# Starting the paired 64-step form two units earlier, in a linear-attention and SwiGLU kernel

## The chip, the cores and the metric

The kernel runs on one core of one Trainium2 chip. The metric is the time of one execution on the device in microseconds (us), taken as the median of several runs. A profile is one further execution, in which each engine's instructions are recorded. Five engines have a queue of their own, worked off in order: TensorE (PE in the profile, its weight loads PEld), VectorE (DVE), ScalarE (ACT), GpSimd (POOL) and SyncE (SP, which here only issues DMAs). Engines wait for each other by semaphores.

## The reference: what is computed

Two blocks follow each other. The first is a recurrence over 768 steps for 4 batches and 8 heads of 48 elements; its output becomes 3072 rows of 384, which go through a gated feed-forward block with 1536 hidden columns.

```python
for t in range(S):
    kt, vt, rt = (k[:, :, t], v[:, :, t], r[:, :, t])
    cur = np.einsum('bhd,bhe->bhde', u[None] * kt, vt)
    y[:, :, t] = np.einsum('bhd,bhde->bhe', rt, state + cur)
    state = w[None, :, :, None] * state + np.einsum('bhd,bhe->bhde', kt, vt)
...
g = x @ w_gate
silu = g * (1.0 / (1.0 + np.exp(-g)))
val = x @ w_val
return (silu * val @ w_out).astype(np.float32)
```

## The kernel before

**Units.** The recurrence is done in chunks. A chunk of one batch needs the products of all pairs of its steps (scores, masked so that only earlier steps count), the sum over these with `v` plus what the state gives (outputs), and the state's own change (update). The work is cut into 24 units of 128 tokens, numbered in the order in which they are done. Before the change, units 0 to 11 are chunks of 128 steps of one batch, the first three chunks of each of the four batches (`c, b = divmod(i, 4)`). Units 12 to 23 have another form, called paired here: 64 steps of two batches, one in partitions 0 to 63 and one in 64 to 127. `PAIRED` is the number of the first paired unit, and `part(i, p)` tells batch and first step of half `p`.

**The two forms on TensorE.** A plain unit has scores in line 494, outputs in line 645 (a product with the state tile `zs` and one with `v`) and the state's update in line 658. A paired unit has scores in line 546, outputs in line 580 (state and `v` lie in the same tile `v_ld`, so one product covers both) and the update in line 594. Each of `v_ld2` and `v_ld3` (printed by the listings of the instructions as `v_ld_107` and `v_ld_108`) holds, in the paired form, 64 steps of `v` of batch 2 or 3 in half of the partitions and that batch's state in the other half.

**The state of a paired unit.** After the update's matmuls, VectorE adds the result onto the state in `v_ld` (line 610, two instructions for each batch), and GpSimd multiplies the state by the decay (line 613, one for each batch). The next unit of the same two batches reads this state in its outputs. From unit 12 on, batches 0 and 1 take turns with batches 2 and 3, so a state that unit `i` leaves is read by unit `i + 2`.

**The order of the work.** A loop over steps `s` issues everything in program order, and each engine works off its own instructions in this order. In step `s` stand, among others:
- at its top, on GpSimd, `scale_k(s+1)` (line 353) and `own_product(s+1)` (lines 264 and 267);
- `gaps(s, 0)` to `gaps(s, 4)`, five places at which pieces of the feed-forward block are issued by `feed`; each piece is a few matmuls with what belongs to them on the other engines;
- between `gaps(s, 0)` and `gaps(s, 1)`, for paired units, `outputs(s-2)`, then `scores(s-1)` with the update of unit `s-2`; for plain units the scores come first.

Small things of the attention are put into queues and taken out one or two at each `feed`: `small` holds ScalarE's instructions for the term with `u`, `lazy` holds the masked copies of the scores (lines 502 and 554), the two transposes of the next unit (`turn_block`, on VectorE) and the four additions with the two multiplications of the state (lines 610 and 613). What is left of both queues is issued before the next step's scores.

**The feed-forward block.** At first it is done plainly (`gate_value`, line 688). From the tenth step on, the projections use sums of weights and of hidden columns that save matmuls: `weight_sum` (line 717), `h_sums` (lines 740 to 745) and `project` (line 768). From the thirteenth on, three groups of weights are combined as well (`in_place` in line 860, `w_forms` in line 887, both on GpSimd, and the matmuls in line 957).

**DMAs of a paired unit.** `move_blocks` issues eight DMAs from SyncE that rearrange `hats` (line 435; a plain unit has four, line 419), `fill_turned` and `fill_own` fill parts of `At` (lines 524 and 530), `load_v` loads `v` (line 153). The state of the plain form is copied once into `v_ld` (line 675).

Of the kernel before, what the change touches and what calls it, by code (L numbers as in the profile page):

```python
# [12 lines left out]
AF = mybir.ActivationFunctionType  # L13
ALU = mybir.AluOpType
AX = mybir.AxisListType
P = 128
# [6 lines left out]
def fast(  # L23
# [25 lines left out]
    B, H, S, D = r.shape  # L49
# [15 lines left out]
    dve, pool, act, pe, sp = nc.vector, nc.gpsimd, nc.scalar, nc.tensor, nc.sync  # L65
# [17 lines left out]
    NR = 2 * FC  # L83
# [15 lines left out]
    def take():  # L99
# [3 lines left out]
    own = zs[:].rearrange("p b x -> p (b x)")[:, 0 : 2 * H * 64].rearrange(  # L103
        "p (i h t) -> p i h t", i=2, h=H
    )
    r_ld = [cst.tile([P, H, D], FP32, name=f"r_ld{i}") for i in range(2)]
    k_ld = [cst.tile([P, H, D], FP32, name=f"k_ld{i}") for i in range(2)]

# [17 lines left out]
            return khat[i][:, :, 0:D], rhat[i % 2][:, :, 0:D]  # L126
        return k_ld[i % 2][:], r_ld[i % 2][:]

    PAIRED = 12

    def part(i, p):

        c, q = divmod(i - PAIRED, 2)
        return 2 * q + p, PAIRED // B * P + 64 * c

    def pieces_of(i):

# [189 lines left out]
    for l in range(7):  # L327
        n = 1 << l
# [19 lines left out]
    def slot(i, h):  # L348

        return h if i % 2 else H - 1 - h  # L350
# [20 lines left out]
    def diagonal(i, on_act=None):  # L371

        du = dus.pop(i)
        if i >= PAIRED:
            small.extend(
                lambda h=h: act.activation(  # L376
                    own[:, i % 2, slot(i, h), :], ident64, AF.Identity, scale=du[:, h : h + 1]
                )
                for h in range(H)
            )  # L380
            return
        on_act = on_act or (HP if i < 4 else H)
        small.extend(
            lambda h=h: act.activation(
                At[i % 2][:, h, :], ident[:], AF.Identity, scale=du[:, h : h + 1]
            )
            for h in range(on_act)
        )
        if on_act < H:
            n = H - on_act  # L390
            pool.tensor_mul(
                At[i % 2][:, on_act:H], ident[:].unsqueeze(1).to_broadcast([P, n, P]),
                du[:, on_act:H].unsqueeze(2).to_broadcast([P, n, P]),
            )
# [88 lines left out]
    lazy = deque()  # L483
# [29 lines left out]
    def both(i):  # L513

        return At[i % 2][:].rearrange("p h t -> p (h t)").rearrange(
            "p (o h t) -> p o h t", o=2, h=H
        )
# [8 lines left out]
    def fill_own(i):  # L526

        for p in range(2):
            here = slice(64 * p, 64 * p + 64)
            act.dma_start(out=both(i)[here, p], in_=own[here, i % 2])  # L530

    def paired_scores(i, ps):

# [769 lines left out]
    summed = []  # L1303
    todo = []

    def feed(n, pops=1):
        for _ in range(n):
            ready = [k for k, (need, _) in enumerate(todo) if need <= done["pool"] + len(summed)]
            if ready:
                todo.pop(ready[0])[1]()  # L1310
            for _ in range(min(len(lazy), 1 + (len(lazy) > 9))):
                lazy.popleft()()
            for _ in range(min(pops, len(small))):
                small.popleft()()
# [22 lines left out]
    def gaps(s, n):  # L1337

        if s not in EARLY:
            if n == 0:  # L1340
                coming = 40 * ((s < 14) + (s < 18)) + 14 * (s < 22)
                share[0] = -(-(len(todo) + coming) // max(25 - s, 1))
            feed(
                share[0] // 5 + (n < share[0] % 5) - (n == 1 and BLOCKS <= s < PAIRED),
                1,
            )
            return
        for what in EARLY[s][n]:
            if what == "R":
                if done["pool"] < NW:  # L1350
                    round_weights()
                elif len(summed) < 4:
                    weight_sum()
            else:
                feed(1, 3)

    share = [0]
    BLOCKS = 10
    LATE = 12
    EARLY = {s: ("" if s < 7 else "R", "F", "R", "F", "RF") for s in range(5, 12)}  # L1360
    EARLY[4] = ("R", "F", "", "F", "F")

    def flush():
# [89 lines left out]
    for s in range(4, N + 2):  # L1453
        if 4 < s <= PAIRED:
            own_sum(s)
        if s == PAIRED:
            diagonal(s)
        late = BLOCKS < s + 1 < N and s % 2 == 0
        if s + 3 == PAIRED:

            for e in range(2):
                rows, o = slice(64 * e, 64 * e + 64), 64 - 64 * e
                act.copy(mask64[rows], mask[rows, 0, 64 * e : 64 * e + 64])
                act.copy(ident64[rows], ident[rows, 64 * e : 64 * e + 64])
                sp.dma_start(out=w64[rows, :, 1 - e], in_=w64[o : o + 64, :, 1 - e])
        if s + 1 == BLOCKS:
            turn(s)
        if s + 1 < N:
            scale_k(s + 1)
            if s < PAIRED and not late:  # L1470
                scale_r(s + 1)
            own_product(s + 1)
            if s + 1 < BLOCKS:
                load_v(s + 1)
            if s < PAIRED and s + 3 < N and not late:
                load(s + 3)
        if s + 1 < BLOCKS:
            turn(s)
        gaps(s, 0)
        if s > N:  # L1480
            outputs(s - 2)
        if 4 <= s - 1 < N:
            flush()
            while lazy:
                lazy.popleft()()
            if s - 2 >= PAIRED:
                outputs(s - 2)
                if s < N:
                    fill_own(s)
            scores(s - 1)  # L1490
            if LATE <= s < PAIRED + 2:
                outputs(s - 2)
                update(s - 2)
                fill_own(s)
            if PAIRED <= s < N:
                load_v(s)
                after_visit(s)
            gaps(s, 1)
        if BLOCKS <= s < PAIRED:
            turn_block(s, 0)  # L1500
            feed(1)
            turn_block(s, 1)
        if late and s < PAIRED:
            scale_r(s + 1)
        if s + 2 == PAIRED:
            sp.dma_start(out=scales[64:P, 1:3], in_=scales[0:64, 1:3])
        if BLOCKS <= s + 1 <= PAIRED:
            move_blocks(s + 1)
            if s + 1 < PAIRED:
                load_v(s + 1)  # L1510
        if late and s < PAIRED:
            load(s + 3)
        gaps(s, 2)
        if 4 <= s - 2 < LATE - 2:
            outputs(s - 2)
            update(s - 2)
        if s >= 5 and s % 2:
            queue((s - 3) // 2)
        if s < PAIRED:
            diagonal(s)  # L1520
        if s - 2 >= 4:
            gaps(s, 3)
        gaps(s, 4)
        if s == 11:
            dve.tensor_tensor(bad, held[:], wcol[:], ALU.not_equal)
            dve.tensor_reduce(badc, bad, axis=AX.X, op=ALU.add)
            dve.memset(ones, 1.0)
        if s == 12:

            n_ps = next_psum(HP, P)  # L1530
            pe.matmul(n_ps[0:1, 0, 0:1], badc, ones, start=True, stop=True)
            act.copy(outside, n_ps[0:1, 0, 0:1])
# [435 lines left out]
```

## Time and profile before

| what | value |
|---|---|
| median of three runs | 583.87 us (582.99 to 584.4) |
| the profiled execution | 584.59 us, of which the recorded span is 582.8 us |
| TensorE busy | 571.9 us, 98% of the span |
| VectorE, ScalarE, GpSimd busy | 426.7, 224.2, 391.5 us |
| chain that ended last | 97% TensorE |
| mean granted TensorE clock | 0.996 |

A timeline row gives the start in us from the span's start, the time of the group, engine and line, operation, output and inputs by the program's names, how many, and in brackets the idle time of the engine before it with what ended it. Successive matmuls overlap at their ends, so what a group costs TensorE is read from its start to the start of the next group, not from its own time. [...]

### The profile page before, as it was taken

The numbers are of one execution on the slowest core, as the hardware profiler recorded it, in microseconds if no ns is written. First come the engines' busy times: TensorE is split into PE (matmuls) and PEld (weight loads), VectorE is DVE, ScalarE is ACT, GpSimd is POOL, SyncE is SP. The second block draws the span as 40 slices with busy tenths as digits, with TensorE's granted clock in tenths as the row PEclk, the third lists the DMA queues.
The fourth block names the chain that finished last, engine by engine and source line by source line (L and its number), as shares of the span: only waits on it lengthen the run. The fifth ranks groups of instructions, "written<-read, shape, count | busy, mean of one in ns | idle before, by whom it ended". The sixth has DMA issues, their size and how long they took to land.

```text
span 582.8 us, 13575 instructions
## 1 busy us (share of the span) xinstructions
PE 571.9 (98%) x5370; PEld 515.8 (89%) x5370; DVE 426.7 (73%) x745; ACT 224.2 (38%) x532; POOL 391.5 (67%) x395
## 2 busy tenths in 40 slices
PE   8899999999999999999999999999999999999996
PEld 7688888899988899988889988899988899988896
DVE  7677887488497789597869587869358877477672
ACT  3568878322354521344431343421143320233310
POOL 6589887999999737979536979527988950010610
PEclk9899999999999999999999999999999999999999
DMA  8978888562535425544324544220200000200002
GB/s 202 229 210 236 225 288 121 68 108 50 117 64 98 75 40 110 124 76 88 63 54 90 122 80 80 50 39 21 55 0 1 0 1 2 55 0 2 2 1 57
DMA packets 151734, 48.09 MB, mean 83 GB/s; under 512 B 139313, under 2 KB 142386, under 8 KB 151666
## 3 DMA queue, kind: packets, MB, share of 16 engines
q1 hardware_dynamic: 147218, 40.69, 33.9%
q10 hardware_dynamic: 4448, 6.49, 4.0%
q8 instruction: 43, 0.70, 0.5%
q14 instruction: 25, 0.20, 0.1%
HBM read 28.31 MB, written 4.72 MB: 57 GB/s over the span
## 4 chain that ended last, share of the span: by engine, by line
PE 97%; DMA 1%; issue 0%; DVE 0%; POOL 0%; ACT 0%; POOLq 0%
PE bank L957 32%; PE bank L768 19%; PE ring L957 13%; PE bank L688 12%; PE bank L1190 8%; PE ring L645 3%; PE ring L580 2%; PE ring L494 2%; PE ring L405 1%; PE ring L546 1%; PE ring L1190 1%; DMA hats<-in_r_dram 1%; PE ring L594 1%; PE ring L658 1%; PE ring L306 1%
## 5 line engine op out<-in xcount | busy, mean ns | idle before, releaser
L981 DVE TENSOR_TENSOR hv<-hv,bank 128x512 f32<-128x512 f32 x132 | 87.8, 682 | 38.5 <-PE bank L957 32.8
L688 PE MATMUL bank<-xT,wgv 128*128 128x256 f32 x288 | 68.3, 392 | 1.7 <-POOL wgv L228 1.5
L957 PE MATMUL bank<-xf,wgv 128*128 128x256 f32 x256 | 65.7, 381 | 0.0
L688 PEld LDWEIGHTS bank<-xT,wgv 128*128 128x128 f32 x288 | 54.3, 193 | 10.4 <-POOL wgv L228 1.7
L981 ACT COPY hv<-bank 128x512 f32<-128x512 f32 x72 | 40.8, 584 | 58.3 <-PE bank L957 52.7
L957 PEld LDWEIGHTS bank<-xf,wgv 128*128 128x128 f32 x256 | 48.0, 190 | 6.8 <-DVE kT L1235 0.6
L1244 POOL TENSOR_TENSOR hv<-At,hats 128x512 f32<-128x512 f32 x8 | 10.2, 1274 | 63.8 <-ACT At L1243 63.8
L988 ACT ACTIVATE hv<-hv 128x512 f32<-128x512 f32 (+2 forms) x36 | 22.7, 633 | 49.0 <-DVE hv L981 49.0
L376 ACT ACTIVATE zs<-mask,du 128x64 f32<-128x64 f32 x96 | 29.8, 346 | 20.4 <-DVE hv L781 9.3
L957 PE MATMUL bank<-xT,wgv 128*128 128x256 f32 x144 | 35.5, 379 | 0.0
L957 PE MATMUL bank<-xT,s 128*128 128x256 f32 x152 | 35.2, 380 | 0.0
L768 PE MATMUL bank<-wt,hs 128*128 128x192 f32 x192 | 34.1, 328 | 0.0
L768 PE MATMUL bank<-wo,hs 128*128 128x192 f32 x192 | 33.8, 326 | 0.0
L745 POOL TENSOR_TENSOR hs<-hv,hs 128x768 f32<-128x768 f32 x6 | 11.2, 1875 | 32.6 <-DVE hs L742 32.6
L768 PE MATMUL bank<-wo,hv 128*128 128x192 f32 x192 | 32.8, 327 | 0.0
L957 PEld LDWEIGHTS bank<-xT,s 128*128 128x128 f32 x152 | 28.7, 190 | 4.2 <-issue 0.2
L887 POOL TENSOR_TENSOR s<-s,wgv 128x256 f32<-128x256 f32 x39 | 30.1, 772 | 2.9
L768 PEld LDWEIGHTS bank<-wo,hv 128*128 128x128 f32 x192 | 31.6, 190 | 0.4
L887 POOL TENSOR_TENSOR s<-s 128x256 f32<-128x256 f32 x39 | 31.3, 802 | 0.9
L768 PEld LDWEIGHTS bank<-wo,hs 128*128 128x128 f32 x192 | 31.7, 190 | 0.2
L768 PEld LDWEIGHTS bank<-wt,hs 128*128 128x128 f32 x192 | 31.4, 190 | 0.2
L887 POOL TENSOR_TENSOR s<-wgv 128x256 f32<-128x256 f32 x39 | 29.6, 776 | 1.8 <-PE bank L768 1.8
(239 smaller groups left out, 1439.8 us busy)
## 6 DMA issues: line engine op xcount, KB each, us to landing
hats<-hats SPq DMA_DIRECT2D x96, 64.0 KB, 2.4
w_bits<-in_moe_w_gate_dram SPq DMA_DIRECT2D x6, 768.0 KB
w_bits<-in_moe_w_val_dram SPq DMA_DIRECT2D x6, 768.0 KB, 6.3
w_bits<-in_moe_w_out_dram SPq DMA_DIRECT2D x6, 768.0 KB, 7.0
At<-zs ACTq DMA_DIRECT2D x24, 128.0 KB, 3.7
At<-rT SPq DMA_DIRECT2D x24, 128.0 KB, 2.3
v_ld<-in_v_dram SPq DMA_DIRECT2D x24, 96.0 KB, 5.1
k_ld<-in_k_dram SPq DMA_DIRECT2D x24, 96.0 KB, 3.9
```

The source lines that it names most:

```text
L376: lambda h=h: act.activation(own[:, i % 2, slot(i, h), :], ident64, AF.Identity, scale=du[:, h : h + 1])
L494: pe.matmul(ps[e][:, a, :], kT[i % 2][rows, at(i, a), :], turned[i][rows, at(i, a), :], start=True, stop=True, skip_group_check=True,)
L580: pe.matmul(ps[32 * q : 32 * q + 32, cc, 64 * p : 64 * p + 64], *x, start=start, stop=stop, skip_group_check=True,)
L645: pe.matmul(ps[32 * q : 32 * q + 32, cc, :], *x, start=start, stop=stop, skip_group_check=True,)
L688: pe.matmul(gv[:, o, :].rearrange("p (i t) -> p i t", i=2), wt[:, c, P * f : P * (f + 1)], xT[:, 2 * g % NX : 2 * g % NX + 2, c, :], start ...
L745: on.tensor_sub(s[1], h12, x["s"][1])
L768: pe.matmul(ps, lhs[:, f, :], rhs[:, f, :], start=(f == 0 and n in (0, 1, 4)), stop=(f == FH - 1), skip_group_check=True,)
L887: op(made[o], made[a], made[b])
L957: pe.matmul(ps[:, o], u[:, o], v, start=first and o == 0, stop=True, skip_group_check=True,)
L981: do(out, *(pair_of(wide[a][:]) if isinstance(a, str) else a for a in args))
L988: todo.append((at, lambda: act.activation(gate, gate, AF.Silu)))
L1190: pe.matmul(ps, (h[what][q] if h[what] is D_ else h[what][:, q])[:, f, :], wide["o"][what][:, f, :], start=first and f == 0 and (split or ...
```

## The change

The paired form begins at unit 10. The third chunk of batches 2 and 3, which was units 10 and 11 of 128 steps of one batch, becomes two units of 64 steps of both batches: unit 10 has the chunk's first half, unit 11 the second. Both are therefore of the same two batches, and unit 11 reads the state that unit 10 leaves. Units 8 and 9 (the third chunk of batches 0 and 1) stay plain, units 12 to 23 stay as they were.

```diff
+    own_first = hv[:, NR : NR + 4].rearrange("p r t -> p (r t)").rearrange(
+        "p (i h t) -> p i h t", i=2, h=H
+    )
+
+    def own_of(i):
+        return (own_first if i < PAIRED + B // 2 else own)[:, i % 2]
...
-    PAIRED = 12
+    PAIRED = 10
     def part(i, p):
-        c, q = divmod(i - PAIRED, 2)
-        return 2 * q + p, PAIRED // B * P + 64 * c
+        if i < PAIRED + B // 2:
+            return 2 + p, PAIRED // B * P + 64 * (i - PAIRED)
+        c, q = divmod(i - PAIRED - B // 2, 2)
+        return 2 * q + p, (PAIRED // B + 1) * P + 64 * c
...
-    def feed(n, pops=1):
+    def feed(n, pops=1, lazies=1):
...
-            for _ in range(min(len(lazy), 1 + (len(lazy) > 9))):
+            for _ in range(min(len(lazy), lazies + (len(lazy) > 9))):
...
-                feed(1, 3)
+                feed(1, 3, 2)
...
-    LATE = 12
+    LATE = 10
     EARLY = {s: ("" if s < 7 else "R", "F", "R", "F", "RF") for s in range(5, 12)}
+    EARLY[10] = EARLY[11] = ("R", "FF", "R", "F", "RF")
...
-        if s + 3 == PAIRED:
+        if s + 1 == PAIRED:
...
             if PAIRED <= s < N:
-                load_v(s)
+                if s == PAIRED + 2:
+                    load_v(s - 1)
+                if s != PAIRED + 1:
+                    load_v(s)
                 after_visit(s)
```

`own_first` is another place for the term with `u`, since the tile used later still holds the plain form's state; the activations and `fill_own` go through `own_of`. Because unit 11 takes over the `v_ld` tiles of unit 10, its `v` is loaded one step later than else. In steps 10 and 11 as many pieces are fed as before; each feed there takes two things out of `lazy`. An own line of the outputs' stores is not changed, but a paired unit stores each half by itself.

What the change makes of the queues is shown at three places. Line numbers from 118 on are higher in the changed kernel, at these places by 9 to 13 (line 613 is 622 there, 353 is 362, 580 is 589, 768 is 777).

TensorE around the begin of step 13, before: the last pieces of step 12, then the scores of unit 12 (the outputs of unit 11 follow them). Names in brackets are the engines and DMA rings that an instruction waits for.

```order
L768 MATMUL bank_95<-wo,hs 128x192 [waits DVE_49]
L768 MATMUL bank_95<-wo,hs 128x192 x5
L957 MATMUL bank_93<-xf,wgv 128x256 [waits Activation_49]
L957 MATMUL bank_93<-xf,wgv 128x256
L546 MATMUL ring_99<-rT,kT_112 64x64 x2
L546 MATMUL ring_96<-rT,kT_112 64x64 x2
```

The same place in the changed kernel: now the outputs of unit 11 come there, in the paired form.

```order
L777 MATMUL bank_95<-wo,hs 128x192 [waits DVE_49]
L777 MATMUL bank_95<-wo,hs 128x192 x5
L966 MATMUL bank_93<-xf,wgv 128x256 [waits Activation_49]
L966 MATMUL bank_93<-xf,wgv 128x256
L589 MATMUL ring_98<-At_111,v_ld_107 32x64 [waits DMAHW4_49,DMAHW2_49,Pool_49]
L589 MATMUL ring_98<-At_111,v_ld_107 32x64
L589 MATMUL ring_98<-At_111,v_ld_107 32x64 [waits DMAHW5_49]
L589 MATMUL ring_98<-At_111,v_ld_107 32x64
L589 MATMUL ring_98<-At_111,v_ld_108 32x64 [waits DMAHW6_49,DMAHW3_49,Pool_49]
```

Two of these wait for GpSimd: for the multiplications of `v_ld2` and of `v_ld3` that unit 10 leaves.

GpSimd at the same place, before: weight combinations (`s`), `scale_r(13)` (`hats<-r_ld`), then the top of step 13.

```order
L887 TENSOR_TENSOR s<-wgv 128x256
L356 TENSOR_TENSOR hats<-r_ld_102,scales 128x8x48
L887 TENSOR_TENSOR s<-s 128x256
L887 TENSOR_TENSOR s<-s,wgv 128x256
L887 TENSOR_TENSOR s<-wgv 128x256
L353 TENSOR_TENSOR hats<-k_ld_103,scales 128x8x48
L264 TENSOR_TENSOR rk<-r_ld_101,k_ld_103 128x384
L267 TENSOR_TENSOR rk<-rk,scales 128x384
L887 TENSOR_TENSOR s<-wgv 128x256
```

In the changed kernel:

```order
L365 TENSOR_TENSOR hats<-r_ld_102,scales 128x8x48
L896 TENSOR_TENSOR s<-wgv 128x256
L896 TENSOR_TENSOR s<-s 128x256
L896 TENSOR_TENSOR s<-s,wgv 128x256
L896 TENSOR_TENSOR s<-wgv 128x256
L622 TENSOR_TENSOR v_ld_107<-v_ld_107,w_82 48x4x2x48
L362 TENSOR_TENSOR hats<-k_ld_103,scales 128x8x48
L273 TENSOR_TENSOR rk<-r_ld_101,k_ld_103 128x384
L276 TENSOR_TENSOR rk<-rk,scales 128x384
L622 TENSOR_TENSOR v_ld_108<-v_ld_108,w_82 48x4x2x48
```

The two multiplications of the state stand behind all weight combinations of step 12, and the second one behind the three instructions of the top of step 13 as well.

VectorE in step 11, before: the masked copy of unit 10 and the two transposes of unit 11, then the additions to the state and the sums of hidden columns (`hs`).

```order
L502 COPY_PREDICATED At0_110<-mask_86,ring3_99 128x4x128
L455 STREAM_TRANSPOSE kT1_113<-hats_109 128x4x128
L455 STREAM_TRANSPOSE rT_1419<-hats_109 128x4x128
L670 TENSOR_TENSOR zs_100<-ring1_97,zs_100 48x4x48 x2
L740 TENSOR_TENSOR hs_1488<-hv_90 128x768
L742 TENSOR_TENSOR hs_1488<-hs_1488,hv_90 128x768
L744 TENSOR_TENSOR hs_1503<-hv_90 128x768
L745 TENSOR_TENSOR hs_1503<-hv_90,hs_1488 128x768
L776 TENSOR_TENSOR hv_90<-hv_90,bank2_94 128x192
```

In the changed kernel:

```order
L284 TENSOR_REDUCE du_1510<-rk_1420 128x8
L466 STREAM_TRANSPOSE kT1_113<-hats_109 128x512
L749 TENSOR_TENSOR hs_1517<-hv_90 128x768
L751 TENSOR_TENSOR hs_1517<-hs_1517,hv_90 128x768
L563 COPY_PREDICATED At0_110<-mask_86,ring3_99 64x256
L466 STREAM_TRANSPOSE rT_1512<-hats_109 128x512
L753 TENSOR_TENSOR hs_1549<-hv_90 128x768
L754 TENSOR_TENSOR hs_1549<-hv_90,hs_1517 128x768
L785 TENSOR_TENSOR hv_90<-hv_90,bank2_94 128x192
```

The first transpose now stands right ahead of the first sum of hidden columns, the second transpose and a masked copy between the sums.

More of the change, by code (lines that the diff above doesn't have):

```diff
@@ L376, in diagonal @@
                 lambda h=h: act.activation(
-                    own[:, i % 2, slot(i, h), :], ident64, AF.Identity, scale=du[:, h : h + 1]
+                    own_of(i)[:, slot(i, h), :], ident64, AF.Identity, scale=du[:, h : h + 1]
                 )
@@ L529, in fill_own @@
             here = slice(64 * p, 64 * p + 64)
-            act.dma_start(out=both(i)[here, p], in_=own[here, i % 2])
+            act.dma_start(out=both(i)[here, p], in_=own_of(i)[here])
     def paired_scores(i, ps):
```

## The prediction

> **What bounds the kernel now.** I read the page's head and its chain of waits first, to know whose time counts; then the idle time of TensorE (PE) after the start phase; then the timelines of the steps that change form and, for GpSimd (POOL), of the steps ahead of the first use of the new state.
>
> ```profile
> span 582.8 us, 13575 instructions
> PE 571.9 (98%) x5370; PEld 515.8 (89%) x5370; DVE 426.7 (73%) x745; ACT 224.2 (38%) x532; POOL 391.5 (67%) x395
> PE 97%; DMA 1%; issue 0%; DVE 0%; POOL 0%; ACT 0%; POOLq 0%
> PE ring L594 <- issue: 0.6, 1, 0.6
> PE ring L957 <- issue: 0.2, 1, 0.2
> ```
>
> The first three lines are the page's; the last two are all waits of PE from 100 us to the end. PE never waits there for another engine, so every us of matmul saved is a us of time, and every us by which another engine now comes too late is lost in full: nothing later can give it back. All sums are made against the profiled execution (584.59 us, span 582.8); it lies 0.72 us above the median of 583.87, and I carry the differences over to the median.
>
> **The change part by part: matmuls.** A plain unit as PE does it (scores, outputs, update, next piece), then a paired one (outputs, scores, update, next piece):
>
> ```profile
> 132.07 1.16 PE L494 MATMUL ring<-rT,kT 48*128 48x128 f32 x16
> 133.17 0.43 PE L645 MATMUL ring<-rT,zs 112*32 112x128 f32 x8
> ...
> 134.73 0.52 PE L658 MATMUL ring<-v_ld,hats 128*32 128x48 f32 x32
> 135.18 2.06 PE L768 MATMUL bank<-wt,hs 128*128 128x192 f32 x11
> ...
> 178.43 1.11 PE L580 MATMUL ring<-At,v_ld 112*32 112x64 f32 x64
> 179.47 0.69 PE L546 MATMUL ring<-rT,kT 48*64 48x64 f32 x32
> 179.99 0.63 PE L594 MATMUL ring<-v_ld,hats 64*64 64x48 f32 x32
> 180.55 1.13 PE L957 MATMUL bank<-xf,wgv 128*128 128x256 f32 x4
> ```
>
> From start to start the plain unit costs 1.10 (scores) + 1.56 (outputs) + 0.45 (update) = 3.11 us, the paired one 0.52 + 1.04 + 0.56 = 2.12. Units 10 and 11 change form, the number of feed-forward pieces stays: 2 x 0.99 = **-1.98 us**.
>
> **The state of unit 10.** Units 12 and later read a state two units after it was made. Unit 11 now reads unit 10's, one step after. Its outputs stand on PE where the scores of unit 12 stand before, at 153.89, and wait for the two multiplications of the state on POOL, which stand behind all weight combinations of step 12 and, for `v_ld3`, also behind the top of step 13. PE first, then POOL, then the same multiplication further on:
>
> ```profile
> 141.14 2.11 PE L768 MATMUL bank<-wo,hs 128*128 128x192 f32 x12
> 143.09 1.14 PE L768 MATMUL bank<-wt,hs 128*128 128x192 f32 x6
> ...
> 153.89 0.69 PE L546 MATMUL ring<-rT,kT 48*64 48x64 f32 x32
> 143.33 2.73 POOL L887 TENSOR_TENSOR s<-wgv 128x256 f32<-128x256 f32 x3 [0.33 <-PE bank L768]
> 146.14 0.72 POOL L887 TENSOR_TENSOR s<-s 128x256 f32<-128x256 f32 x1
> ...
> 152.62 0.73 POOL L887 TENSOR_TENSOR s<-wgv 128x256 f32<-128x256 f32 x1
> 153.31 1.00 POOL L353 TENSOR_TENSOR hats<-k_ld,scales 128x384 f32<-128x384 f32 x1
> 154.27 1.00 POOL L264 TENSOR_TENSOR rk<-r_ld,k_ld 128x384 f32<-128x384 f32 x1
> 155.35 1.01 POOL L267 TENSOR_TENSOR rk<-rk,scales 128x384 f32<-128x384 f32 x1
> 156.32 0.72 POOL L887 TENSOR_TENSOR s<-wgv 128x256 f32<-128x256 f32 x1
> 197.87 0.83 POOL L613 TENSOR_TENSOR v_ld<-v_ld,w 48x384 f32<-48x384 f32 x1 [1.90 <-DVE v_ld L610]
> ```
>
> Both engines can be counted from one event. POOL's combinations begin when PE's project of 141.14 has ended (143.09): POOL had waited 0.33 us for it. From there POOL needs 0.24 (to 143.33), 9.98 (to 153.31: eleven weight combinations and `scale_r`), 0.91 for `v_ld2` (0.83 and a step to the next instruction as between its neighbours), 3.01 (to 156.32: the top of step 13) and 0.83 for `v_ld3`: 14.97 us, and some 0.1 until PE sees it. PE needs 153.89 - 143.09 = 10.80 for the pieces up to the outputs, and the pieces don't change. So the outputs of unit 11 stand still for 15.07 - 10.80 = 4.27 us: a short first wait of 0.5 for `v_ld2`, then, after the four matmuls (under 0.1 us) that need only this, the rest for `v_ld3`. I take **+4.2 us**. Before the change PE has none of it. The gain does not shorten it: four of the six changed groups (less the update's loss) come ahead of the project of 141.14 and move the common event by 2 x 0.58 + 0.52 - 0.11 = 1.57 us on both engines, if POOL keeps up. The rows speak for that: the plain multiplications of `zs`, one pair of which goes (below, 1.26 us), stand ahead of the event.
>
> Bounds: with all combinations at the 0.72 us of the row at 146.14 instead of up to 0.91 (2.73 for three), POOL is 1.0 earlier: 3.2. With all at 0.91, 1.1 later: 5.3. I take the middle, since it is the row of these very instructions in this place.
>
> **The clock.** What a stall of this length does besides is seen at the start of the span. Columns: window, its length; busy time of PE, PEld, DVE, ACT, POOL with instructions; granted PE clock; DMA share, GB/s. Below, the same twelve matmuls right behind the gap and later.
>
> ```profile
> 13.42:16.83 3.41, 3.08 (x71) 2.23 (x68) 3.38 (x7) 3.41 (x8) 0.48 (x1) 1.00 0.89 172
> 16.83:20.24 3.41, 0.91 (x7) 0.44 (x5) 2.43 (x6) 2.56 (x8) 1.88 (x2) 1.00 0.79 153
> 20.24:23.65 3.41, 3.26 (x10) 2.66 (x11) 1.81 (x4) 0.00 (x0) 3.41 (x5) 0.65 1.14 285
> 20.39 4.54 PE L688 MATMUL bank<-xT,wgv 128*128 128x256 f32 x12 [1.45 <-POOL wgv L228]
> 26.83 2.86 PE L688 MATMUL bank<-xT,wgv 128*128 128x256 f32 x12
> ```
>
> A stretch of 3.41 us with 2.50 us idle is followed by one with a granted clock of 0.65, and twelve matmuls take 4.54 instead of 2.86: 1.68 us lost. The stretch before, with 0.33 idle, had no such follower. If the clock is judged in such stretches, a wait of 3.8 us puts 2.5 us or more into one of them when it begins in the first 0.91 or the last 1.3 to 1.4 us of a stretch, about 0.67 of all positions; if less idle than 2.5 is enough (the trace leaves 0.33 to 2.5 open), in more: with 2.0, nearly all. I take three in four. The price is 1.68 where the slow stretch begins behind the wait and 1.0 to 1.4 where its first part still lies in the wait: **+1.4**, between 0 and 1.7.
>
> [...]
>
> **The sum.** 583.87 - 1.98 + 4.2 + 1.4 = 587.5 us.
>
> **What I cost at nothing**, with its cover. Unit 11 has eight DMAs of blocks on SP instead of four, and they stand behind the two that fill `At` with unit 10's transposed block:
>
> ```profile
> 109.58 3.99 SPq L419 DMA_DIRECT2D hats<-hats  x4
> 194.67 5.42 SPq L435 DMA_DIRECT2D hats<-hats  x8
> hats<-hats SPq DMA_DIRECT2D x96, 64.0 KB, 2.4
> 167.15 0.69 DVE L457 STREAM_TRANSPOSE kT<-hats 128x512 f32<-128x512 f32 x1
> 123.06 0.97 DVE L740 TENSOR_TENSOR hs<-hv 128x768 f32<-128x768 f32 x1
> 124.07 1.15 DVE L742 TENSOR_TENSOR hs<-hs,hv 128x768 f32<-128x768 f32 x1
> 126.13 2.11 PE L768 MATMUL bank<-wt,hs 128*128 128x192 f32 x12
> ```
>
> Before, the four were issued from 109.58. Now the eight can begin at about 114.5 (my estimate: some 4.9 us later, for unit 10's second transpose and the two fills) and land by 114.5 + 5.42 + 2.4 = 122.3; then follow unit 11's first transpose (0.69) and the two sums of hidden columns (0.97 and 1.15): about 125.1, against 125.5 when PE wants them (126.13 less 0.6 already gained). The cover is 0.4 us; gone, the price is at most the 5.42 - 3.99 = 1.43 by which the issue grew. The masked copies and transposes of a paired unit, its activations and its stores lie beside PE's pieces on engines that are 38 to 73% busy. The state copies of batches 2 and 3 and the late loads of `v` on SP, and all else that SP does later in steps 8 to 10, meet POOL, which has room there only in stretches; its whole room is this:
>
> ```profile
> 102.28:156.32 54.04, 54.04 (x648) 50.15 (x650) 34.43 (x54) 16.49 (x53) 51.22 (x50) 1.00 0.48 83
> 139.89 1.26 POOL L671 TENSOR_TENSOR zs<-zs,w 48x192 f32<-48x192 f32 x2
> ```
>
> **The rivals.** *A, predicted: wait and slow stretch*, 587.5.
>
> *B, the wait, but the clock holds*: 587.5 - 1.4 = 586.1. For it speaks that the wait is cut in two by the four matmuls, and the position of a stretch's border, which I can't know; against it the row with 0.91 us of work.
>
> *C, the other side: POOL's multiplications are there in time*, and the matmul gain stands alone: 583.87 - 1.98 = 581.9. It decides when POOL is 4.2 us earlier at its `v_ld3` than I count, against PE's common event. Against it: from 102.28 to 156.32 POOL was busy 51.22 of 54.04 us, so even without a single wait (2.82) and with the `zs` pair gone (1.26), but with 0.91 and 0.83 for the new multiplications, it would be done at 156.32 - 2.82 - 1.26 + 0.91 + 0.83 = 153.98, still 1.7 behind the 152.32 (153.89 - 1.57) at which PE comes. Only much faster combinations could make it.
>
> *D, a short stall*: POOL's combinations are free of the wait for the project and POOL works without a pause; the stall is the 1.7 just worked out, too short for the clock: 583.87 - 1.98 + 1.7 = 583.6, no change to be measured.
>
> *E, a further wait ahead of the stall*: SP's longer queue makes the sums of hidden columns late. From 0.4 us of delay on PE waits there too, up to 1.43 - 0.4 = 1.0: 588.5.
>
> **How the numbers follow.** Chances: A 0.58 and B 0.22, three to one with some room for the border; C 0.08; D 0.07; E 0.05. The time is A's, 587.5. The low end is B with the stall at its lower bound (586.1 - 1.0 = 585.1) and 0.5 for the spread of a median (the runs lie between -0.9 and +0.5 of theirs): 584.6; the high end is A with the stall at 5.3 (+1.1) and the full 1.68 (+0.3), and 0.5: 589.4. C and D lie outside, 0.15. What a measurement of this kernel can tell from no change is about 0.2%, 582.70 to 585.04: faster is C, 0.08; the same is D, 0.07; slower are A, B and E, 0.85.
>
> **What would show it right or wrong in the profile after.** Matmuls: outputs, scores and update of units 10 and 11 at 1.04, 0.52 and 0.56 us from start to start. Stall: a wait of PE's line 589 (580 before) for POOL's line 622 (613 before), once, 3 to 5 us, near 152 us of the span, and the only one of its size behind 100 us; POOL's `v_ld3` row right behind the three of the top of step 13. If POOL's first combination no longer waits for PE, D is nearer. Clock: a granted clock of about 0.6 to 0.8 in a stretch of 3.41 us right behind the wait, and PE's matmuls there at up to double their time; if it is 1.00, B. E: a wait of line 777 (768 before) for VectorE near 125 us. The prediction falls if the wait is under 2 us, or if PE's wait names another engine than POOL: VectorE's last addition to `v_ld3` (line 610) is the next that could be late.

## The result, and the profile after

| what | before | after |
|---|---|---|
| median | 582.47 us (6 runs, 581.55 to 584.4) | 590.67 us (6 runs, 589.34 to 594.17) |
| ratio to the kernel before, 95% interval | | 1.015, 1.0113 to 1.0187 |
| profiled execution | 584.59 us, span 582.8 | 589.34 us, span 587.5 |

The change makes the kernel slower, by 8.2 us where 3.6 were predicted. The predicted time of 587.5 us and the end of its range, 589.4, are both too low, although the prediction was made against 583.87 and the median of all runs of the kernel before turned out to be 582.47 (580.8 to 581.1 beside the experiments below). The profile of before is one of its longer executions: up to 25 us its start takes 2.9 us more than in the profile of after. Counted from the feed-forward piece behind that start, which begins at 26.83 us before and at 23.95 after, to the last matmul, the two profiles differ by 7.1 us.

The page's head and all waits of TensorE from 60 us to the end, in the profile after:

```profile
span 587.5 us, 13712 instructions
PE 571.3 (97%) x5418; PEld 515.2 (88%) x5418; DVE 427.5 (73%) x753; ACT 223.1 (38%) x532; POOL 393.6 (67%) x395
PE ring L589 <- POOL v_ld L622: 3.7, 2, 3.6
PE bank L777 <- DVE hs L751: 1.4, 1, 1.4
PE ring L603 <- issue: 0.9, 1, 0.9
PE ring L654 <- ACT kT L418: 0.4, 1, 0.4
PE bank L697 <- DVE hv L704: 0.2, 1, 0.2
```

Before, only "issue" stood there (0.8 us in all). Now there are four waits for other engines: for the state (3.7), for a sum of hidden columns (1.4), and two small ones, at 90 and 95 us. In the timelines each matmul has two records (16 matmuls that are added further down stand there as x32), so x8 are four matmuls. The timeline of TensorE at unit 10's outputs, where nothing is waited for, and at unit 11's:

```profile
124.88 2.19 PE L777 MATMUL bank<-wt,hs 128*128 128x192 f32 x12 [1.38 <-DVE hs L751]
...
131.21 1.11 PE L589 MATMUL ring<-At,v_ld 112*32 112x64 f32 x64
132.25 0.69 PE L555 MATMUL ring<-rT,kT 48*64 48x64 f32 x32
132.77 0.63 PE L603 MATMUL ring<-v_ld,hats 64*64 64x48 f32 x32
133.33 0.92 PE L777 MATMUL bank<-wt,hs 128*128 128x192 f32 x4
...
152.26 0.32 PE L589 MATMUL ring<-At,v_ld 112*32 112x64 f32 x8 [0.16 <-POOL v_ld L622]
156.15 1.72 PE L589 MATMUL ring<-At,v_ld 128*32 128x64 f32 x56 [3.56 <-POOL v_ld L622]
157.80 1.13 PE L555 MATMUL ring<-rT,kT 48*64 48x64 f32 x32
158.71 1.05 PE L603 MATMUL ring<-v_ld,hats 64*64 64x48 f32 x32
159.69 2.71 PE L966 MATMUL bank<-xf,s 128*128 128x256 f32 x8
162.23 2.11 PE L966 MATMUL bank<-xT,s 128*128 128x256 f32 x9
```

Unit 10's outputs, scores and update take 1.04, 0.52 and 0.56 us, 2.12 in all, as predicted. The same work of unit 11, behind the wait, takes 1.65 for seven eighths of the outputs, then 0.91 and 0.98. GpSimd's queue shows why the wait has its length, the windows why the work behind it is slow (columns as in the prediction's windows):

```profile
141.48 2.46 POOL L896 TENSOR_TENSOR s<-wgv 128x256 f32<-128x256 f32 x3 [2.03 <-PE bank L777]
...
151.38 0.83 POOL L622 TENSOR_TENSOR v_ld<-v_ld,w 48x384 f32<-48x384 f32 x1
152.29 1.00 POOL L362 TENSOR_TENSOR hats<-k_ld,scales 128x384 f32<-128x384 f32 x1
...
155.27 0.82 POOL L622 TENSOR_TENSOR v_ld<-v_ld,w 48x384 f32<-48x384 f32 x1
151.00:154.40 3.40, 1.43 (x14) 0.81 (x12) 0.71 (x2) 0.59 (x1) 3.17 (x5) 0.99 0.88 185
154.40:157.80 3.40, 1.66 (x57) 1.49 (x57) 0.00 (x0) 0.00 (x0) 3.24 (x5) 0.50 0.63 97
157.80:161.20 3.40, 3.40 (x72) 3.04 (x69) 0.00 (x0) 0.48 (x1) 3.24 (x5) 0.51 0.44 99
161.20:164.60 3.40, 3.40 (x17) 2.99 (x16) 2.61 (x5) 0.44 (x1) 3.24 (x6) 1.00 0.48 81
```

The half clock lasts for two stretches of 3.4 us, not one: the first of them still holds 1.74 us of the wait. (By the trace's record of the clock it is half from 154.33 to 161.16, so the borders of these windows are 0.08 us or less off.) The work from 156.15 to 162.23 takes 6.08 us. At full clock it is 0.91 + 0.52 + 0.56, and 1.84 for the x8 group of line 966 (from a kernel below that has no slow clock), 3.83 in all. The clock costs 2.25 us.

### The profile page after: what moved, and what is told of

It is laid out like the page before. It is cut to its first block, busy times and chain, and to the rows that moved or that the text cites. A ratio compares the mean times of both kernels' runs of the same rounds, so it can differ in the third digit from the quotient of the medians.

```text
span 587.5 us, 13712 instructions
## 1 busy us (share of the span) xinstructions
PE 571.3 (97%) x5418; PEld 515.2 (88%) x5418; DVE 427.5 (73%) x753; ACT 223.1 (38%) x532; POOL 393.6 (67%) x395
## 4 chain that ended last, share of the span: by engine, by line
PE 82%; POOL 6%; ACT 4%; DVE 3%; SPq 2%; issue 1%; DMA 1%; POOLq 0%; DVEq 0%; ACTq 0%
PE bank L966 31%; PE bank L777 16%; PE ring L966 13%; PE bank L1199 8%; PE bank L697 4%; PE ring L589 3%; PE ring L555 2%; POOL wgv L261 2%; POOL s L896 1%; PE ring L1199 1%; PE ring L603 1%; ACT bank L213 1%; DMA w_bits<-in_moe_w_out_dram 1%; SPq L444 1%; ACT w_low L219 1%
## 5 line engine op out<-in xcount | busy, mean ns | idle before, releaser
L697 PE MATMUL bank<-xT,wgv 128*128 128x256 f32 x288 | 66.6, 385 | 1.9 <-POOL wgv L237 1.5
L966 PE MATMUL bank<-xT,wgv 128*128 128x256 f32 x144 | 35.5, 379 | 0.0
```

Of the source, the lines that this page charges most:

```text
L697: pe.matmul(gv[:, o, :].rearrange("p (i t) -> p i t", i=2), wt[:, c, P * f : P * (f + 1)], xT[:, 2 * g % NX : 2 * g % NX + 2, c, :], start ...
L966: pe.matmul(ps[:, o], u[:, o], v, start=first and o == 0, stop=True, skip_group_check=True,)
```

## The experiments

All medians below are taken beside runs of the kernel before on the same chip, in four sessions: 580.8 us in the first, which ran on one chip, and 581.03, 581.08 and 580.91 in the others, on a second chip. An interval of a ratio is about 0.1 to 0.3% to each side, 0.5 to 1.8 us; smaller differences are read from profiles.

**The changed kernel once more, and its two waits taken away, singly and together.** First the kernel unchanged:

> The changed kernel once more, unchanged, timed against the kernel before, for the part of the loss that one profile does not explain. The profile shows -2.0 us of matmuls, 3.7 us of waiting for GpSimd's multiplications of the state, 1.4 us of waiting for VectorE's sum of hidden columns and about 2.5 us of half clock behind the first wait: +5.6 us, where the medians differ by 8.2. If the 2.6 us are a varying number of slow clock stretches, the times are 588 to 594 and the longer ones have the lower mean clock (0.992 for 589 to 591, 0.986 for 594). If they are work of the kernel, the difference is 8 us in every round at a clock of 0.992.

590.36 us, ratio 1.0162 (1.0135 to 1.0189), at clocks of 0.989 to 0.995. The profile shows the same waits: 3.6 for the state, 1.4 for the sum, 0.9 and 0.2 near 90 us. So the loss is the kernel's, and no accident of one session.

The state earlier (in `paired_update`):

```diff
         for p in range(2):
             for g in range(2):
-                lazy.append(lambda p=p, g=g: add(p, g))
+                if i == PAIRED:
+                    add(p, g)
+                else:
+                    lazy.append(lambda p=p, g=g: add(p, g))
```

> The changed kernel with the four additions and two multiplications that make unit 10's state issued at once behind its update, instead of one by one behind the later pieces; nothing else moves. They then stand on GpSimd in front of the last two of the in-place sums of weights, and GpSimd has 2.0 us of idle time right behind. Theory (the wait makes the slow clock): both go, 3.7 + 2.5 = 6.2 us less than the changed kernel, about 584.5 us, and no stretch under a clock of 0.9 behind 100 us. Rival (the clock falls at this place for another reason): 3.7 us less, 587.0 us. Rival (another engine is late next, for instance VectorE's masked copies behind the four additions): a new wait of 1 to 3 us of TensorE for VectorE between 133 and 155 us.

584.67 us, ratio 1.006 (1.0036 to 1.0085): 5.7 us less, where the theory said 6.2 and the rival 3.7. GpSimd now does both multiplications ahead of its combinations, where it had idled 2.03 us, and no idle time is left there:

```profile
137.26 2.37 POOL L622 TENSOR_TENSOR v_ld<-v_ld,w 48x384 f32<-48x384 f32 x2
...
141.33 2.46 POOL L899 TENSOR_TENSOR s<-wgv 128x256 f32<-128x256 f32 x3
```

No wait for the state is left in its profile, and the mean clock is 0.999; from 100 to 200 us it is 1.00, where the changed kernel has 0.97. The wait and the slow clock went together.

The sums first (in `after_visit`):

```diff
+        if s == PAIRED + 1:
+            lazy.extend([
+                *masked[:2], own_term, lambda: None,
+                lambda: turn_block(s, 0), turn_second, *masked[2:], *sums,
+            ])
+            return
```

> The changed kernel with the first transpose of unit 11 issued behind the first two sums of hidden columns instead of ahead of them; the second transpose and the fills follow it, the third and fourth masked copy of unit 10 come behind. Theory (the sum is late only because it stands behind a transpose that waits for the eight DMAs): TensorE's wait of 1.4 us for VectorE goes, and GpSimd can follow, since it idles 2.0 us before the event that both count from: 1.4 us less than the changed kernel, about 589.3 us. Rival (GpSimd can't follow): the wait for the state grows by as much, and the time stays at 590.7 us.

587.3 us, ratio 1.0105 (1.008 to 1.0129): 3.1 us less, where 1.4 were expected. VectorE in the changed kernel, and then in this one:

```profile
121.29 0.71 DVE L466 STREAM_TRANSPOSE kT<-hats 128x512 f32<-128x512 f32 x1 [1.51 <-DMA hats<-hats]
121.92 1.14 DVE L749 TENSOR_TENSOR hs<-hv 128x768 f32<-128x768 f32 x1
123.10 1.63 DVE L751 TENSOR_TENSOR hs<-hs,hv 128x768 f32<-128x768 f32 x1
```

```profile
118.73 0.94 DVE L755 TENSOR_TENSOR hs<-hv 128x768 f32<-128x768 f32 x1
119.71 1.15 DVE L757 TENSOR_TENSOR hs<-hs,hv 128x768 f32<-128x768 f32 x1
120.97 0.71 DVE L466 STREAM_TRANSPOSE kT<-hats 128x512 f32<-128x512 f32 x1
```

The transpose had waited 1.51 us for the blocks' DMAs with the sums queued behind it. The sums themselves were also longer there, 2.77 us instead of 2.09. The wait for the state stays (3.9 us), since GpSimd follows. This profile has no wait near 90 us either, although the edit touches nothing that early, so part of the 3.1 us may not be the edit's.

Both edits:

> Both edits in the changed kernel. Theory: no wait and no slow stretch is left, and the matmul gain stands alone: 582.5 - 2.0 = 580.5 us, faster than the kernel before by 0.34%. Rival (the 2.6 us that the profile does not explain are work of the new form itself, on any engine): 583 us, no faster than before.

582.08 us, ratio 1.0019 (1.0002 to 1.0035): 0.2% slower than the kernel before, where 580.5 were expected. The rival's number is nearer, but not its cause: TensorE's waits from 60 us on show two for ScalarE:

```profile
PE bank L975 <- ACT hv L999: 1.9, 1, 1.9
PE ring L663 <- ACT kT L418: 1.3, 1, 1.3
PE ring L609 <- issue: 0.5, 1, 0.5
PE bank L706 <- DVE hv L713: 0.2, 1, 0.2
```

The second stands near 90 us, ahead of everything that the two edits touch. The first, at 167 us, is in its profiled execution of 584.82, the longest of the twelve runs; it is followed by a clock of 0.77 and 0.73.

**Where the wait near 90 us comes from.** Outputs of a plain unit, which write `ring`, wait there for ScalarE's copy of a transpose out of `ring` (0.4 us in the changed kernel's profile). ScalarE is late because it waited 2.12 us for weights. SP's issues in the changed kernel, then before, then ScalarE in the changed kernel:

```profile
77.08 1.29 SPq L156 DMA_DIRECT2D k_ld<-in_k_dram  x2
78.42 2.27 SPq L156 DMA_DIRECT2D r_ld<-in_r_dram  x2
80.79 0.57 SPq L193 DMA_DIRECT2D w_bits<-in_moe_w_out_dram  x1
81.46 0.52 SPq L1519 DMA_DIRECT2D scales<-scales  x1
82.07 0.54 SPq L193 DMA_DIRECT2D w_bits<-in_moe_w_out_dram  x1
85.18 1.42 SPq L684 DMA_DIRECT2D v_ld<-zs  x2
86.69 0.55 SPq L193 DMA_DIRECT2D w_bits<-in_moe_w_out_dram  x1
```

```profile
79.91 0.37 SPq L147 DMA_DIRECT2D k_ld<-in_k_dram  x1
80.33 0.57 SPq L147 DMA_DIRECT2D r_ld<-in_r_dram  x1
81.00 3.52 SPq L184 DMA_DIRECT2D w_bits<-in_moe_w_out_dram  x3
```

```profile
86.29 0.52 ACT L213 ACTIVATE bank<-w_bits 128x384 f32<-128x384 f32 x1 [2.12 <-DMA w_bits<-in_moe_w_out_dram]
```

From its first load to the first weights SP took 1.09 us before and takes 3.71 now; a copy of the table `scales` and the two copies of unit 6's state stand among the weights. Three things that the change lengthens or moves are thus ahead of the weights. In the next kernel the loads and the state copies are put behind the weights of their step (the table stays):

```diff
-            if s < PAIRED and s + 3 < N and not late:
+            if s < PAIRED and s + 3 < N and not late and s not in (7, 8):
                 load(s + 3)
...
         gaps(s, 4)
+        if s in (7, 8):
+            load(s + 3)
+            while copies:
+                copies.popleft()()
```

(`update` puts unit 6's two copies into `copies` instead of issuing them.)

> The kernel with both edits, and SP's queue changed in steps 7 and 8: the loads of k and r of units 10 and 11, which the change makes four DMAs each instead of two, and unit 6's two state copies stand behind the three transfers of weights of their step instead of ahead of them. Theory (the longer queue brings the weights late, ScalarE waits 3 us for them and TensorE 0.4 to 1.3 us for ScalarE near 90 us): that wait goes, ScalarE's idle time before line 213 near 86 us falls from 2 to 3 us to under 1, and the time falls by 1.0 to 1.6 us from 582.1, to 580.5 to 581.1; with the wait gone, the matmul gain of 2.0 us should leave 579 if nothing else is late. Rival (the wait comes from ScalarE's or GpSimd's own work): 582.1, unchanged.

579.88 us beside 581.03, ratio 0.9976 (0.9957 to 0.9994): faster than the kernel before, and 2.2 us less than without this edit in the session before. All that TensorE waits for from 60 us on:

```profile
PE ring L610 <- issue: 0.7, 1, 0.7
PE bank L979 <- ACT hv L1003: 0.3, 1, 0.3
```

ScalarE does not wait for the weights there. Why the edit brought more than the 1.0 to 1.6 expected is not shown: the later wait is 0.3 here instead of 1.9, but the 1.9 stood in the longest run alone that was profiled, and that it is in the other runs too was not seen.

The same edit in the changed kernel alone:

> The changed kernel with that change of SP's queue alone. Theory: 1.0 to 1.6 us less than the changed kernel (590.4), about 589; the wait for the state and the wait for the sum of hidden columns stay. Rival: 590.4, since TensorE's wait for GpSimd's state, later on, takes up whatever is gained earlier (then the wait of 3.6 us grows to 5).

586.98 us, ratio 1.0107 (1.0077 to 1.0136): about 3 us less than the 590.4, where 1.0 to 1.6 were expected. The 590.4 are of another session and chip, and four single runs of the unchanged kernel further down took 586.1 to 588.4, so the size is not shown. The profile shows that the wait near 90 us is gone and that the wait for the state is 3.55, not 5, against the rival: GpSimd counts from an event of TensorE and moves with it.

One part alone, in the kernel before: k and r of units 10 and 11 loaded in halves.

```diff
+            for rows, b, t in halves_of(i) if i in (10, 11) else pieces_of(i):
```

> The kernel before with one part of the change alone: k and r of units 10 and 11 are loaded by two DMAs of 64 rows each instead of one of 128, so four issues more on SP for each unit's pair, ahead of the weights; all computation is as before. Theory: SP issues the weights 2.6 us later, ScalarE waits for them near 86 us, and TensorE waits 0.3 to 1.3 us near 90 us: 581.1 to 582.1 us. Rival (the late weights come from the state copies or the table of scales that the change also moves ahead): 580.8 us, no change.

581.73 us, ratio 1.0012 (0.9995 to 1.0029): inconclusive by time. The profile speaks for the rival: SP issues the weights later (83.15 instead of 81.00), but TensorE has no wait between 60 us and the end except "issue". In this profile the loads alone were not enough. That the copies are needed as well is likely but not shown by one profile, since the kernel with the sums first has all three things ahead of the weights and no wait in its profile either.

**The slow clock.** The changed kernel, with idle matmuls in the place of the wait:

```diff
         ps = next_psum(CC, P)
+        if i == PAIRED + 1:
+            for x in range(28):
+                pe.matmul(ps[:, x % CC, :], ident[:], ident[:], start=True, stop=True,
+                          skip_group_check=True)
```

> The changed kernel with 28 idle matmuls of 128 x 128 (the identity with itself, into the bank that unit 11's outputs overwrite) ahead of unit 11's outputs, so that TensorE works for some 3.5 us where it otherwise waits for the state. The multiplications of the state come no earlier. Theory (the half clock behind is set off by TensorE's own idle time): the outputs begin when they did, the stretches behind have a clock of 1.00, and the time falls by 2.5 us from 590.4 to 587.9. Rival (the half clock has another cause, such as the load on the memory at this place): 590.4, or a little more.

589.68 us, ratio 1.0159 (1.0128 to 1.019): no gain, but the 28 matmuls, estimated at 3.5 us, took 6.34, more than the wait. In the profile the granted clock was 1.00 throughout, so the mechanism held and the size was wrong. With 16:

> The changed kernel with 16 idle matmuls instead of 28 ahead of unit 11's outputs: the 28 took 6.34 us (0.227 each), 2.2 us more than the wait that they fill; 16 take 3.6. Theory (TensorE's idle time sets off the half clock): clock of 1.00 behind, a remaining wait of under 0.5 us, and 2.2 us less than with 28, about 587.5 us, 2.5 to 3 us less than the changed kernel. Rival: the clock falls again behind this shorter wait, and the time is that of the changed kernel, 590.4.

585.61 us beside 581.08, ratio 1.0082 (1.0063 to 1.0102): nearly 5 us less than the changed kernel in the first session, where 2.5 to 3 were expected. The profiles hold half of it: from the piece behind the start to the last matmul it is 555.6 us here and 558.1 in the changed kernel. The state comes no earlier, 0.2 us of the wait is left, and the work behind it runs at full clock:

```profile
151.69 3.73 PE L576 MATMUL ring<-ident 128*128 128x128 f32 x32
...
155.90 1.00 PE L593 MATMUL ring<-At,v_ld 128*32 128x64 f32 x56 [0.22 <-POOL v_ld L626]
156.83 0.69 PE L555 MATMUL ring<-rT,kT 48*64 48x64 f32 x32
157.34 0.63 PE L607 MATMUL ring<-v_ld,hats 64*64 64x48 f32 x32
157.90 1.99 PE L970 MATMUL bank<-xf,s 128*128 128x256 f32 x8
159.74 2.75 PE L970 MATMUL bank<-xT,s 128*128 128x256 f32 x12
152.40:155.80 3.40, 3.28 (x36) 2.99 (x34) 0.00 (x0) 0.08 (x1) 3.32 (x4) 1.00 0.70 135
155.80:159.20 3.40, 3.30 (x126) 3.03 (x127) 0.06 (x1) 0.48 (x1) 3.17 (x6) 1.00 0.75 149
```

From 155.90 to 159.74 are 3.84 us, where the changed kernel needs 6.08 for the same. With 0.2 us of idle time there in the place of 3.7, the granted clock was 1.00 instead of 0.50: TensorE's own idle time set off the half clock here, since only matmuls in its place were added.

**What the profile does not hold.** The terms read from the profile add up to less than the medians differ by, and the kernel with the early state varies most (581.5 to 587.7 us). Three more profiles of the kernel with the early state, and four of the changed one:

> The kernel with the early state once more, one look with a profile. Its twelve runs lay between 581.5 and 587.7 us at nearly full clock, and its profile was one of the short ones. The kernels in which the sums of hidden columns stand ahead of the transpose spread by 1.6 us. Theory (the eight DMAs that the transpose waits for land at times that vary from run to run): in a run of over 584 us TensorE's wait for the sum of hidden columns is longer than the 1.37 us of the profile by as much as the run is longer. Rival: the wait is 1.4 us again, and the time lies ahead of 60 us, in the start.

> The same kernel, a second look, expected as the first: over 584 us only with a wait for the sum of hidden columns that is longer than 1.37 us; the rival puts the difference into the start.

> The same kernel, a third look, expected as the first: a longer run has a longer wait for the sum of hidden columns; the rival puts the difference into the start.

584.19, 582.89 and 582.89 us. The wait for the sum was 2.01, 2.01 and 1.34, with followers of 0.59, 0.59 and 0.05; the wait near 90 us was 0.52, 0.92 and 0.32. So the wait varies, by some 1.2 us with what follows it, though none of these is one of the runs of 586 to 588. In the second and third a longer wait and an earlier start came out at the same time: the theory is right in part, and neither wait nor start explains the spread alone. Nor do the DMAs explain the longer wait alone: counted from when TensorE wants the sum, the transpose begins 0.2 us later in the first profile than in the third, but the first sum behind it takes 1.74 us instead of 0.99.

> The changed kernel unchanged, one look with a profile. Theory A (the slow clock behind the wait for the state lasts one to four windows): a run of over 591 us has more than 3 us of it where the profiles so far have 2.6 to 2.9. Theory B (the DMAs ahead of the transpose land late): the wait for the sum of hidden columns is 2 us or more instead of 1.4. Theory C: the start up to 60 us is 2 to 4 us longer than in the short runs.

> The same kernel, a second look, with the same three theories: slow clock behind the wait (over 3 us in a long run), the wait for the sum of hidden columns (2 us or more), or the start.

> The same kernel, a third look, with the same three theories: slow clock behind the wait (over 3 us in a long run), the wait for the sum of hidden columns (2 us or more), or the start.

> The same kernel, a fourth look, with the same three theories: slow clock behind the wait (over 3 us in a long run), the wait for the sum of hidden columns (2 us or more), or the start.

586.14, 586.89, 588.4 and 587.18 us on another chip, beside one run of the kernel before of 580.88. The wait for the state was 3.68, 3.37, 3.37 and 3.69; the wait for the sum 1.33, 2.00, 2.04 and 1.36; the slow clock, from the end of the wait to the second group of line 966 against 3.84, cost 1.5, 1.6, 2.9 and 1.4 us. Theories A and B each hold in part: between these runs the clock makes up to 1.5 us and the sum up to 0.7. Theory C holds between sessions: the piece behind the start begins at 22.7 to 23.0 us in these four, at 23.95 in the profile of the result and at 25.52 in that of the repeated kernel, the longest (590.72 us), whose start has a half clock from 19.71 to 23.12. From that piece to the last matmul all six take 556.3 to 558.1 us, the kernel before 551.0. None of the four was as long as the medians in the other sessions.

**The single term again, and the best kernel again.**

> The changed kernel with the early state and SP's changed queue, but with the transpose of unit 11 ahead of the sums of hidden columns as in the changed kernel. Theory: only TensorE's wait for VectorE's sum is left, 1.4 us and 0.4 us of followers: 1.8 us more than the kernel with all three edits, 581.7 us where that has 579.9. Rival (the wait varies with the landing of the eight DMAs and is larger in most runs): 2.6 to 3.1 us more, 582.5 to 583.0.

581.51 us, ratio 1.0002 (0.9988 to 1.0016): 1.7 us more than the next kernel, where the theory said 1.8. The number agrees better than its make-up: this profile has three waits for VectorE (1.4, 0.5 and 0.4), and the next kernel has one for ScalarE at 164 us (0.3, and slower matmuls behind it) that this one has not.

> The kernel with all three edits once more, to see whether it beats the kernel before again. Theory: matmuls -2.0 us, one wait of 0.3 us left: 0.2 to 0.3% less than before, 579.4 to 580. Rival: the first comparison was chance, and the two are equal within 0.1%.

579.84 us beside 580.91, ratio 0.9981 (0.9972 to 0.999). The kernel with all three edits beats the kernel before a second time, by 0.2%.

## Why the prediction was wrong, step by step

Three terms failed: the size of the clock's, and two waits that were put at nothing. The matmuls and the wait for the state came out.

- **Matmuls, -1.98 us: right.** Unit 10 costs 2.12 us from start to start. What is left of it in the kernel with all edits is 1.1 us in both comparisons, with intervals that reach from 0.3 to 2.5 and from 0.6 to 1.6.
- **The wait for the state, +4.2: right in place, cause and size.** 3.7 us of waiting, and the first four matmuls of the outputs took 0.3 us within, where the prediction has under 0.1. GpSimd's path from its common event with TensorE is 14.91 us, predicted 15.07. The 0.1 us in it until TensorE sees the end was an estimate; in the profile after it is 0.06 (156.09 to 156.15). In the profile after GpSimd idles 2.03 us just ahead of this event (0.33 before); the multiplications could have stood there.
- **The clock, +1.4 between 0 and 1.7: the mechanism right, the size wrong.** The step that failed is that one slow stretch follows, for 1.68 us at most. The wait of 3.6 us lies across a border, and the second stretch, which holds 1.74 us of it, was followed by another at half clock. It cost 2.25 in the profile and 1.4 to 2.9 in the repeats. It differs from run to run: of the profile after and its four repeats two show it for about two stretches (2.25 and 2.9 us) and three for one (1.4 to 1.6), as predicted. The prediction's stretches were also not the clock's own. By its record the clock is half from 21.29 to 24.71 there, and the stretch ahead of it, from 17.88, has 1.56 us of work, so 1.85 us of idle time, not only the 2.50 that were read, were followed by the half clock. In the profile after, a stretch with 1.43 us of work in 3.40 was followed by the half clock, and the next, with 1.66, by another at half.
- **The sums of hidden columns, costed at nothing with 0.4 us of cover: wrong.** This was rival E, to which the prediction gave 0.05, with up to 1.0 us. The transpose began at 121.29, about 1.1 later than worked out (122.3, less the 2.1 us by which the profile is ahead there); and the two sums took 0.65 us more than their rows before. Together 1.75, less the cover 1.35; the wait was 1.38, and followers made it about 1.8. The sum's error was to take two estimates in a row as exact against a cover of 0.4.
- **SP's longer queue in steps 7 to 10, costed at nothing: wrong.** The prediction looked for its cover on GpSimd. The chain ran over ScalarE: loads and copies ahead of the weights, ScalarE waiting 2.1 us for these, TensorE waiting for ScalarE's copies and then for VectorE, 0.6 us in the profile and 0.4 to 1.6 in others (none in the kernel with the sums first alone). With the loads and state copies behind the weights it is in none of four profiles.
- **The base.** The sum began at the median of three runs, 583.87; over six it was 582.47. Relative to that the predicted 3.6 would have given 586.1, so the base hid part of the error in the time.

From the profile: 3.7 (state) + 2.25 (clock) + 1.8 (sum) + 0.6 (near 90 us) - 1.98 = 6.4 us. Between the two profiles 7.1 are to be explained, so 0.7 are in no term. The measured 8.2 has an interval of 6.6 to 10.9, and the four repeats lie 5.3 to 7.5 above their one run of before. That the medians of two sessions lie at the upper end is left open: start, clock and sum vary by enough, but no profile shows a run over 590.72.

## What to carry to other kernels

When an edit shortens the distance between where a value is made and where it is read, count both engines' queues from their last common event, as this went right to 0.2 us; then put the producer into the first gap ahead of it. When an edit adds DMAs to an issuing queue, ask what else stands in that queue, who waits for it, and who waits for that one: the cover has to be found on the engine at the end of the chain. The cover of 0.4 us that rested on two estimates was none. The wait of 3.4 to 3.6 us of TensorE cost 1.4 to 2.9 us more behind it in five profiles.

## What the hardware showed unexpectedly

In the profiles before and after, the record of TensorE's clock has the half clock for 3.41 us (from 21.29, before) and for 6.83 (from 154.33, after), and once more at the end of both. Cut into stretches of 3.41 us from these two starts, back and forth, the stretches at full clock with 0.18 and 1.56 us of work before, and with 1.04 and 1.51 after (as the profile counts TensorE's busy time), were followed by the half clock. Of the others at full clock from 14 us on the least work was 2.51 us before and 2.01 after, and none of them was. At half clock, the stretch with 1.60 us of work (from 154.33, after) was followed by another at half, the two with 3.41 (from 21.29 before and 157.74 after) by full clock. The waits of 2.0 us for the sum in the second and third repeat left the clock at 1.00, from 120.30 to 133.95.

Where VectorE's two sums and GpSimd's instructions ran beside each other, either could take longer than elsewhere. In the changed kernel the sums took 2.77 us and `scale_r` beside them 1.71, where it took 1.02 at 110.39. Before, the sums took 2.12 and the two multiplications of `zs` beside them 1.68, where two took 1.08 in the changed kernel. In the kernel with the sums first, the sums took 2.09.
